# Two memsets moved, a third copy of the channel weights built by TensorE, and one weight load cut into seven

## The chip, the cores and the metric

The kernel runs on one core of a Trainium2 chip. The metric is the device time of one execution in microseconds; the figure given is the median of three runs. A profile of one further execution is used to say where the time goes; its times count from the start of its span.

## The reference

A causal convolution of seven taps, softmax-normalised and one set per head, is followed by a spectral mixing of the lowest 64 Fourier modes and a channel product with a ReLU:

```python
w = softmax(weight)                            # [8 heads, 7 taps]
x = causal_conv(x, w)                          # [8, 3264, 192], 24 channels a head
X = np.fft.rfft(x, axis=1)[:, :64]
Yr = Xr @ w_r - Xi @ w_i                       # per mode, 192x192
Yi = Xr @ w_i + Xi @ w_r
y = irfft(Yr + 1j*Yi, n=3264)                  # the other modes are zero
u = x + y
out = u + np.maximum(u @ w_ch, 0.0)            # w_ch is 192x192
```

All inputs and the output are float32; inside, the kernel works with bf16 operands and float32 accumulators.

## The kernel before

**Stages.** First, the taps are computed (VectorE and ScalarE, L231 to L241), TensorE spreads them into band matrices (L244), and copies put these into the tile `bandyet` (L249 to L253), which L187 has set to zero. Second, the convolution: the eight sequences are taken in four pairs, each in three units (`UNITS`), the last rows first. TensorE multiplies by the band matrices (L316 to L324), ScalarE and VectorE write the result back over `xall` (L331, L333), TensorE adds each finished unit to its Fourier transform with tables made on the fly (L341), and the result is transposed into `xt` (L355). The last 64 partitions of the last tile of every pair do not exist in the input; L188 sets them to zero. Third, the mixing: 16 groups of four modes. `mix(g)` (L463) multiplies `xt` by the weights of group g, 12 matmuls on L470. Between the groups, `some(3)` takes three bank jobs from a list, transposes by TensorE (L419, L429) with a copy each (L405, L407) that prepare tables `gt` and the transposed input `ct`; every second group ends in `mix_trans` (L485). Fourth, 52 output tiles: matmuls on L509, a ReLU (L539), an addition (L547) and a store by SP (L551).

**Channel weights.** `wm` holds rows 0 to 127 of `w_ch` and, in its columns 192 to 383, an identity; `w1` holds rows 128 to 191 and the remainder of that identity, on partitions 64 to 127. A third tile, `wch`, holds the same weights interleaved: partition p has rows 3p, 3p+1 and 3p+2, once on partitions 0 to 63 and once more on 64 to 127. The lower half is loaded (L284) and `spread_w` (L504, L505) copies it up by one VectorE copy of 64x576, called behind the mixing of groups 0 and 1. `wch` is first read by `z_c(0)`, ahead of the mixing of group 14.

**Order of the loads.** Every load of x and of weights is issued by POOL in the order of the program, since it turns float32 into bf16 on the way. The mixing weights of a group are two loads, real (w_r) into partitions 0 to 63 and imaginary (w_i) into 64 to 127 of a slot, of 288 KB each as written. Seven slots are used by 16 groups, so `load_free` issues the loads of a later group when the mixing that frees its slot has been written out: group 7's behind `mix(0)`, group 9's behind `mix(2)`, group 15's behind `mix(8)`. The program has 65 POOL loads: 30 of x, 3 of channel weights, 32 of mixing weights. Their completion is counted in eight semaphores, given out in turn (DMASW0 to DMASW7 in the built program), and each load waits, before it is issued, for the load that used its semaphore last, the eighth before it. Loads are called below by their part and group: r9 is w_r of group 9, i9 is w_i of group 9.

**Copies.** `copy` (L402) sends its second and fourth call of every five to ScalarE, the others to VectorE; `next_bank` (L409) turns through four PSUM banks.

Of the kernel before, what the change touches and what calls it, by code (L numbers as in the profile page):

```python
# [17 lines left out]
def kernel(  # L18
# [11 lines left out]
    nc = tc.nc  # L30
    B, S, D = x.shape
# [5 lines left out]
    P = 128  # L37
    NQ = B // 2
    NB = 13
# [25 lines left out]
    def sb(name, shape, dtype):  # L65
        return pool.tile([P] + shape, dtype, tag=name, name=name)
# [5 lines left out]
    xall = sb("xall", [NQ, NB, 2, 2, D], BF16)  # L72
# [5 lines left out]
    bandyet = sb("bandyet", [2 * H * P], BF16)  # L78
# [4 lines left out]
    wm = sb("wm", [2 * D], BF16)  # L83
    w1 = sb("w1", [2 * D], BF16)
    wch = sb("wch", [3, D], BF16)
# [7 lines left out]
    def wgroup(flat):  # L93
        return flat.rearrange("p (m j e) -> p m j e", m=4, j=3)

    slots = [wgroup(ct[:, 3, WGB * i:WGB * (i + 1)]) for i in range(4)]
    slots += [wgroup(arena[:, WGB * i:WGB * (i + 1)]) for i in range(NA)]
    NG = MODES // 4
    slot_of = [4, 5, 0, 1, 2, 3, 6, 4, 5, 0, 1, 2, 3, 6, 4, 5]
# [84 lines left out]

    blank = gt[:, :, :, :].rearrange("p h t s -> p (h t s)")[:, 0:512]
    nc.vector.memset(blank, 0.0)
    nc.vector.memset(bandyet[:], 0.0)  # L187
    nc.vector.memset(xall[64:P, :, NB - 1, 1, :, :], 0.0)  # L188
    nc.vector.memset(halfpi[:], math.pi / 2)
    nc.vector.memset(tiny, 0.0)  # L190
    nc.vector.memset(ascale[:], 2.0 / S)
# [2 lines left out]
    def active(n, bank, left, right):  # L194

        for _ in range(n):
            nc.tensor.matmul(bank[:, :], left, right, start=True, stop=True, skip_group_check=True)
# [41 lines left out]
    nc.vector.tensor_scalar(out=wsum[k7, :], in0=wsum[k7, :], scalar1=1e-9, scalar2=None, op0=ALU.add)  # L239
    nc.vector.reciprocal(out=wrec[k7, :], in_=wsum[k7, :])  # L240
    nc.vector.tensor_tensor(out=taps_t[k7, :], in0=wexp_t[k7, :], in1=wrec[k7, :], op=ALU.mult)  # L241

    for i in range(2 * PW):
        nc.tensor.matmul(xtrb[0:32, H * i:H * i + H], shift[k7, 2 * PW - 1 - i:2 * PW + 31 - i], taps_t[k7, :],  # L244
                         start=(i == 0), stop=True, tile_position=(0, 0), skip_group_check=True)
    for g in range(4):
        dst = band[32 * g:32 * g + 32, :, :, 16 * g:16 * g + PW]
        if g == 0:
            nc.vector.tensor_copy(out=dst, in_=xtrb[0:32, 0:2 * PW * H].rearrange("p (c e h) -> p e h c", e=2, h=H))  # L249
        elif g == 2:  # L250
            nc.scalar.copy(out=dst, in_=band[0:32, :, :, 0:PW])
        else:
            nc.vector.tensor_copy(out=dst, in_=band[0:32, :, :, 0:PW])  # L253
    active(6, dftb, blank[:, 0:P], blank)
    PIECES = ((18, 26), (10, 18), (0, 10))
    table_dve(*PIECES[0], (0, 1, 2))
# [24 lines left out]
        load_unit(*u)  # L281
    nc.gpsimd.dma_start(out=wm[:, 0:D], in_=moe_w_ch[0:P, :])
    nc.gpsimd.dma_start(out=w1[64:P, 0:D], in_=moe_w_ch[P:D, :])
    nc.gpsimd.dma_start(out=wch[0:64, :, :], in_=moe_w_ch.rearrange("(p j) e -> p j e", j=3))  # L284

    def load_w(g):
        for half, src in ((0, moe_w_r), (1, moe_w_i)):
            nc.gpsimd.dma_start(out=slots[slot_of[g]][64 * half:64 * half + 64, :, :, :],
                                in_=src[4 * g:4 * g + 4, :, :].rearrange("m (p j) e -> p m j e", j=3))

    loaded = [0]

    def load_free(mixed):
        while loaded[0] < NG:
            before = [g for g in range(loaded[0]) if slot_of[g] == slot_of[loaded[0]]]
            if before and before[-1] >= mixed:
                break
            load_w(loaded[0])
            loaded[0] += 1
# [102 lines left out]
    def copy(out, in_):  # L402
        ncopy[0] += 1
        if ncopy[0] % 5 in (2, 4):
            nc.scalar.copy(out=out, in_=in_)  # L405
        else:
            nc.vector.tensor_copy(out=out, in_=in_)  # L407

    def next_bank():  # L409
        k = tbank[0] % 4  # L410
        tbank[0] += 1
        return single[k][:, :]
# [44 lines left out]
    def some(n):  # L457
        for _ in range(n):
            if tjobs:
                f, *a = tjobs.pop(0)  # L460
                f(*a)

    def mix(g):  # L463
        last = g >= NG - 2
        yp = yps[g % 2][:, 0:D] if last else yps[(g // 2) % 2][:, D * (g % 2):D * (g % 2) + D]
        w = slots[slot_of[g]]
        for j in range(3):
            for p4 in range(4):
                m = 4 * g + p4
                nc.tensor.matmul(yp[32 * p4:32 * p4 + 2 * B, :], xt[:, j, :, m], w[:, p4, j, :],  # L470
                                 start=(j == 0 and (last or g % 2 == 0)), stop=(j == 2),
                                 tile_position=(0, 32 * p4), skip_group_check=True)
        mixed[0] = g
        load_free(g + 1)

    def mix_copy(d):
        nc.scalar.copy(out=ymix[d % 2][:], in_=yps[d % 2][:, 0:2 * D].rearrange("p (g d) -> p g d", g=2))
# [3 lines left out]
    def mix_trans(d):  # L481
        et = ets[d % 2][:, 0:256].rearrange("p (t g k) -> p t g k", t=2, g=2)
        for t in range(2):
            for g in range(2):
                nc.tensor.matmul(et[:, t, g, :], ymix[d % 2][:, g, 64 * t:64 * t + P], used, start=True,  # L485
                                 stop=True, skip_group_check=True)
        for t in range(2):
            yet_copy(d, t, et[:, t, :, :])
# [12 lines left out]
    def height(t):  # L501
        return P if t < NB - 1 else LASTM

    def spread_w():  # L504
        nc.vector.tensor_copy(out=wch[64:P, :, :], in_=wch[0:64, :, :])  # L505

    def z_mm(zt, e, i, l, r, begin, end):
        bank = zt[i] if isinstance(zt, list) else zt[:, i, :]
# [66 lines left out]
    for d in range(ND - 2):  # L575
        mix(2 * d)
        some(3)
        mix(2 * d + 1)
        mix_copy(d)
        some(3)  # L580
        mix_trans(d)
        if d == 0:
            spread_w()
        if d == 3:
            tjobs[5:5] = [(zw_job, q) for q in range(NQ)]
    d = ND - 2
# [80 lines left out]
    n = N - 1  # L667
# [6 lines left out]
    m = height(items[n][1])  # L674
# [38 lines left out]
```

## Time and profile before

| | |
|---|---|
| median of three runs | 175.78 us (175.54 to 175.99) |
| the profiled execution | 176.01 us |
| its span | 174.2 us, so 1.8 us lie outside it |
| granted TensorE clock | 0.993 |
| busy: PE, DVE, ACT, POOL | 157.3, 113.3, 98.4, 50.2 us |
| POOL's loads (q0, "software_dynamic") | 35600 packets, 19.62 MB |
| stores (q1, "hardware_dynamic") | 13934 packets, 20.06 MB |
| transfers of kind "instruction" on q8 | 24 packets of 16 KB |

The page cuts the span into 40 slices of 4.4 us; a digit is the busy share of a slice in tenths. POOL's loads run from 3 us to 105.7 us of the span, the stores from 111 us to the end. The groups, waits and timelines of the profile tell which instruction waited for what. Beside these the trace holds one row for each DMA packet (start, duration, size, queue, but not which of the 16 DMA engines moved it), and the time of each completion mark: each POOL load leaves sixteen, one by each DMA engine when its share has been written. A load has landed with its sixteenth mark.

### The profile page before, as it was taken

Reading aid. Unit: us, or ns where it says so; the run is one execution under the profiler, and the core shown is the slowest. Engines: PE = TensorE matmul, PEld = TensorE weight load, DVE = VectorE, ACT = ScalarE, POOL = GpSimd, SP = SyncE. Lnnn points to the kernel's source line nnn. Section 1 sums busy time; section 2 is a strip of 40 time slices with the busy share of each in tenths; the row PEclk is TensorE's granted clock in tenths of the full one; section 3 lists DMA queues with packets and bytes.
Section 4 is the critical chain, followed back from the end, with each engine's and each line's share of the span. In section 5 each row is a group of like instructions: output and inputs, shape, how many; then the busy total and the mean of one; then the engine's idle time right before and its main releaser. Section 6 shows DMA issues by size and latency. Waiting matters only on the chain.

```text
span 174.2 us, 7009 instructions
## 1 busy us (share of the span) xinstructions
PE 157.3 (90%) x3103; PEld 135.1 (78%) x3104; DVE 113.3 (65%) x158; ACT 98.4 (56%) x139; POOL 50.2 (29%) x82
## 2 busy tenths in 40 slices
PE   7669867999999999899999787999999999999970
PEld 2366746678888887688887774899999999999960
DVE  6697744254535435576775653887888888888880
ACT  3454737424444442658778572776667766676640
POOL 7985795444223642056444000000000000000000
PEclk9999999999999999999999999999999999999997
DMA  2999999999999999999999990299999999999985
GB/s 20 190 191 192 189 193 192 193 192 193 191 192 192 204 208 206 206 206 206 206 207 206 206 169 8 93 346 317 336 336 352 344 320 348 344 332 341 338 314 191
DMA packets 49627, 40.12 MB, mean 230 GB/s; under 512 B 28285, under 2 KB 49597, under 8 KB 49597
## 3 DMA queue, kind: packets, MB, share of 16 engines
q0 software_dynamic: 35600, 19.62, 81.1%
q1 hardware_dynamic: 13934, 20.06, 32.7%
q8 instruction: 24, 0.39, 0.8%
q14 instruction: 6, 0.05, 0.1%
q10 hardware_dynamic: 63, 0.00, 0.0%
HBM read 39.23 MB, written 20.05 MB: 340 GB/s over the span
## 4 chain that ended last, share of the span: by engine, by line
PE 71%; DMA 19%; POOL 4%; issue 2%; ACT 1%; DVE 1%; DVEq 0%; POOLq 0%
DMA xall<-in_x_dram 12%; PE x_right L341 9%; PE z_right L509 9%; PE zb_left L509 8%; PE zs L509 8%; PE zt L509 8%; PE w_left L429 7%; DMA arena<-in_moe_w_i_dram 6%; PE x_left L316 5%; PE x_left L321 3%; PE w_right L470 2%; PE x_right L316 2%; POOL xall L143 2%; PE w_left L419 2%; PE x_left L324 2%
## 5 line engine op out<-in xcount | busy, mean ns | idle before, releaser
L509 PEld LDWEIGHTS <-gt 64*128 64x128 bf16 (+1 forms) x832 | 35.5, 96 | 1.7 <-issue 1.5
L316 PEld LDWEIGHTS <-bandyet 128*64 128x64 bf16 x384 | 26.3, 110 | 11.2 <-issue 11.2
L316 PE MATMUL x_left<-xall,bandyet 128*64 128x192 bf16 (+1 forms) x256 | 25.6, 253 | 5.7 <-DMA xall<-in_x_dram 4.9
L333 DVE CAST xall<-x_left 128x768 bf16<-128x768 f32 (+1 forms) x16 | 16.1, 1007 | 18.6 <-PE x_left L324 13.3
L509 PEld LDWEIGHTS <-ct 64*128 64x128 bf16 (+1 forms) x624 | 26.5, 96 | 0.9 <-DVE ct L407 0.4
L143 POOL DMA_DIRECT2D xall<-in_x_dram x24 | 21.6, 909 | 13.2 <-DMA xall<-in_x_dram 12.5
L331 ACT CAST xall<-x_left 128x768 bf16<-128x768 f32 (+1 forms) x16 | 13.4, 838 | 20.2 <-PE x_left L324 20.2
L324 PE MATMUL x_left<-xall,bandyet 128*64 128x192 bf16 (+1 forms) x128 | 24.4, 251 | 0.0
L321 PE MATMUL x_left<-xall,bandyet 128*64 128x192 bf16 x128 | 23.7, 246 | 0.0
L321 PEld LDWEIGHTS <-bandyet 128*64 128x64 bf16 x192 | 21.1, 110 | 0.1
L324 PEld LDWEIGHTS <-bandyet 128*64 128x64 bf16 x192 | 21.1, 110 | 0.0
L407 DVE COPY ct<-w_left 128x1024 bf16<-128x1024 bf16 x24 | 15.9, 689 | 7.3 <-PE w_left L429 4.3
L429 PE MATMUL w_left<-ident,xall 128*128 128x128 bf16 x312 | 19.6, 220 | 0.0
L341 PE MATMUL x_right<-xall,fz 128*128 128x384 bf16 (+1 forms) x104 | 19.0, 327 | 0.0
L429 PEld LDWEIGHTS <-xall 128*128 128x128 bf16 x312 | 17.6, 103 | 1.7
L405 ACT COPY ct<-w_left 128x1024 bf16<-128x1024 bf16 (+1 forms) x16 | 15.2, 961 | 4.9 <-PE w_left L429 3.1
L333 DVE CAST xall<-x_right 128x768 bf16<-128x768 f32 (+1 forms) x8 | 8.5, 1057 | 9.9 <-PE x_right L324 7.7
L341 PEld LDWEIGHTS <-fz 128*128 128x128 bf16 (+1 forms) x104 | 9.4, 98 | 7.0 <-issue 0.7
L316 PE MATMUL x_right<-xall,bandyet 128*64 128x192 bf16 (+1 forms) x128 | 13.7, 257 | 0.8 <-DMA xall<-in_x_dram 0.8
L539 ACT ACTIVATE z_right<-z_right 128x768 f32<-128x768 f32 (+1 forms) x13 | 10.3, 794 | 4.8 <-PE z_right L509 4.3
L509 PE MATMUL zb_left<-fz,gt 64*128 64x192 bf16 (+1 forms) x208 | 13.0, 243 | 0.0
L324 PE MATMUL x_right<-xall,bandyet 128*64 128x192 bf16 (+1 forms) x64 | 13.0, 256 | 0.0
(130 smaller groups left out, 299.3 us busy)
## 6 DMA issues: line engine op xcount, KB each, us to landing
out_dram<-arena SPq DMA_DIRECT2D x25, 384.0 KB, 3.8
xall<-in_x_dram POOLq DMA_DIRECT2D x24, 384.0 KB, 12.4
out_dram<-xt SPq DMA_DIRECT2D x12, 384.0 KB, 3.7
out_dram<-ct SPq DMA_DIRECT2D x10, 384.0 KB, 3.5
arena<-in_moe_w_r_dram POOLq DMA_DIRECT2D x8, 288.0 KB, 10.4
arena<-in_moe_w_i_dram POOLq DMA_DIRECT2D x8, 288.0 KB, 10.3
ct<-in_moe_w_r_dram POOLq DMA_DIRECT2D x8, 288.0 KB, 9.9
ct<-in_moe_w_i_dram POOLq DMA_DIRECT2D x8, 288.0 KB, 10.7
```

What stands on the lines that cost most here:

```text
L143: nc.gpsimd.dma_start(out=dst, in_=src)
L316: nc.tensor.matmul(cols[r, :, e, :].rearrange("p t (i d) -> p t i d", i=2), band[:, e, h, 0:64], xall[:, q, t0:t0 + n, half, :, dsl], star ...
L321: nc.tensor.matmul(cols[0:64, b0:n, e, :].rearrange("p t (i d) -> p t i d", i=2), band[:, e, h, 64:P], xall[:, q, t0 + b0 - 1:t0 + n - 1, ...
L324: nc.tensor.matmul(cols[64:P, :, e, :].rearrange("p t (i d) -> p t i d", i=2), band[:, e, h, 64:P], xall[:, q, t0:t0 + n, 0, :, dsl], star ...
L331: nc.scalar.copy(out=dst, in_=srcv)
L333: nc.vector.tensor_copy(out=dst, in_=srcv)
L341: nc.tensor.matmul(xp, ftab[0:r, 2 * t + e, :], xall[0:r, q, t, e, :, :].rearrange("p i d -> p (i d)"), start=(t == UNITS[0][0] and e == 0 ...
L405: nc.scalar.copy(out=out, in_=in_)
L407: nc.vector.tensor_copy(out=out, in_=in_)
L429: nc.tensor.transpose(tp[:, P * k:P * k + P], src, ident[:])
L509: nc.tensor.matmul(bank[0:l.shape[-1], D * e:D * e + D], l, r, start=begin, stop=end, tile_position=(64 * i, 0), skip_group_check=True)
L539: nc.scalar.activation(out=zt[0:m, :, 0:2 * D], in_=zt[0:m, :, 0:2 * D], func=ACT.Relu)
```

## The change

Three edits:

1. The memset of `bandyet` moves from the head of VectorE's program to behind the last instruction of the taps (L241), and the memset of the missing rows of `xall` to behind the band copies (L253).
2. The load of `wch` and the copy in `spread_w` go. `channel_w`, called in the same place, makes `wch` from `wm` and `w1`: twelve matmuls whose stationary operand is every third column of the identity, over two PSUM banks, then two calls of `copy` (128x384 and 128x192).
3. r9 is issued as seven loads: its first three modes in one, and the rows of its fourth mode in six loads of 15, 14, 12, 10, 8 and 5 partitions.

```diff
     nc.vector.memset(blank, 0.0)
-    nc.vector.memset(bandyet[:], 0.0)
-    nc.vector.memset(xall[64:P, :, NB - 1, 1, :, :], 0.0)
...
     nc.vector.tensor_tensor(out=taps_t[k7, :], in0=wexp_t[k7, :], in1=wrec[k7, :], op=ALU.mult)
+    nc.vector.memset(bandyet[:], 0.0)
...
             nc.vector.tensor_copy(out=dst, in_=band[0:32, :, :, 0:PW])
+    nc.vector.memset(xall[64:P, :, NB - 1, 1, :, :], 0.0)
...
     nc.gpsimd.dma_start(out=w1[64:P, 0:D], in_=moe_w_ch[P:D, :])
-    nc.gpsimd.dma_start(out=wch[0:64, :, :], in_=moe_w_ch.rearrange("(p j) e -> p j e", j=3))
 
     def load_w(g):
         for half, src in ((0, moe_w_r), (1, moe_w_i)):
-            nc.gpsimd.dma_start(out=slots[slot_of[g]][64 * half:64 * half + 64, :, :, :],
-                                in_=src[4 * g:4 * g + 4, :, :].rearrange("m (p j) e -> p m j e", j=3))
+            n = 3 if g == 9 and half == 0 else 4
+            w = slots[slot_of[g]][64 * half:64 * half + 64, :, :, :]
+            nc.gpsimd.dma_start(out=w[:, 0:n], in_=src[4 * g:4 * g + n, :, :].rearrange("m (p j) e -> p m j e", j=3))
+            if n == 4:
+                continue
+
+            a = 0
+            for r in (15, 14, 12, 10, 8, 5):
+                nc.gpsimd.dma_start(out=w[a:a + r, 3, :, :],
+                                    in_=src[4 * g + 3, 3 * a:3 * (a + r), :].rearrange("(p j) e -> p j e", j=3))
+                a += r
...
-    def spread_w():
-        nc.vector.tensor_copy(out=wch[64:P, :, :], in_=wch[0:64, :, :])
+    def channel_w():
+
+        for js in ((0, 1), (2,)):
+            bank = next_bank()
+            for a, j in enumerate(js):
+                for i in range(2):
+                    for k, w in ((slice(0, P), wm), (slice(64, P), w1)):
+                        nc.tensor.matmul(bank[64 * i:64 * i + 64, D * a:D * a + D], w[k, D + j:2 * D:3], w[k, 0:D],
+                                         start=(a == 0 and w is wm), stop=(w is w1),
+                                         tile_position=(0 if w is wm else 64, 64 * i), skip_group_check=True)
+            copy(wch[:, js[0]:js[-1] + 1, :].rearrange("p j e -> p (j e)"), bank[:, 0:D * len(js)])
...
         if d == 0:
-            spread_w()
+            channel_w()
```

## The prediction

> **What bounds the kernel.** I read the page's slices first, then the chain of work that ended last, then the windows around the end of the loads, then POOL's timeline. In the page, DMA is at 9 from 4 us to 105 us, then nearly idle for two slices, then full again with the stores:
>
> ```profile
> DMA  2999999999999999999999990299999999999985
> ```
>
> The chain of work that ended last, cut to 88 to 112 us, ends its first part on a load:
>
> ```profile
> 93.35 0.61 POOL arena L288
> ...
> 94.53 11.20 DMA arena<-in_moe_w_i_dram
> 105.73 0.04 issue
> 105.77 0.47 PE w_right L470 x12
> ```
>
> i15 lands at 105.73 and the last mixing starts at once. From there to the end (174.2 - 105.73 = 68.47 us) the chain is TensorE's and the change touches none of it. So I forecast the landing of i15, and whether TensorE is ready for it. TensorE's timeline shows how far it is ahead:
>
> ```profile
> 97.17 0.45 PE L470 MATMUL w_right<-ct,xt 128*16 128x192 bf16 x12 [0.88 <-DMA ct<-in_moe_w_i_dram]
> 104.74 0.45 PE L470 MATMUL w_right<-arena,xt 128*16 128x192 bf16 x12
> 105.77 0.45 PE L470 MATMUL w_right<-arena,xt 128*16 128x192 bf16 x12 [0.58 <-DMA arena<-in_moe_w_i_dram]
> ```
>
> It waits 0.88 us for i12 and 0.58 us for i15; without waiting it needs 97.17 to 105.19 between them. The windows show that the sixteen DMA engines do not end together (next to last column DMA share, full at 1.21):
>
> ```profile
> 102.00:103.00 1.00, 0.50 (x16) 0.35 (x16) 0.64 (x2) 0.87 (x2) 0.00 (x0) 1.00 1.18 200
> 103.00:104.00 1.00, 1.00 (x22) 0.79 (x23) 0.00 (x0) 0.31 (x1) 0.00 (x0) 1.00 0.69 116
> 104.00:105.00 1.00, 1.00 (x30) 0.84 (x29) 0.29 (x1) 0.27 (x1) 0.00 (x0) 1.00 0.35 67
> 105.00:106.00 1.00, 0.42 (x24) 0.27 (x12) 0.00 (x0) 0.32 (x1) 0.00 (x0) 1.00 0.07 10
> ```
>
> The completion marks of i15 say the same: the first at 103.08, twelve by 104.36, four at 105.43 to 105.73. The first mark of r9 is at 84.47, so an engine does the 13 loads from i9 to i15 in 103.08 - 84.47 = 18.61 us, 1.43 a load. The late engines are those that a 16 KB transfer of kind "instruction" (q8; at 78.97, 85.25, 92.00, 98.45 us) went through: with each, one engine's marks move back by about 1.1 us and stay there.
>
> POOL's timeline shows what lets a load be issued:
>
> ```profile
> 78.48 0.61 POOL L288 DMA_DIRECT2D ct<-in_moe_w_r_dram  x1 [0.73 <-PE w_right L470]
> 79.08 0.62 POOL L288 DMA_DIRECT2D ct<-in_moe_w_i_dram  x1
> ...
> 88.80 0.61 POOL L288 DMA_DIRECT2D arena<-in_moe_w_i_dram  x1 [0.40 <-DMA ct<-in_moe_w_i_dram]
> ```
>
> 78.48 and 79.08 are r9 and i9, behind mix(2); 88.80 is i13, 0.28 after the last mark of i9, eight loads earlier, at 88.52. The same holds for i14 (91.68 after 91.40) and i15 (94.53 after 94.24). Eight loads in flight are 11.4 us of stock, so this never leaves an engine without work.
>
> **Edit 1, the zeros.** At the head VectorE has
>
> ```profile
> 1.30 0.91 DVE L187 MEMSET bandyet<- 128x1024 uint32 x1 [0.16 <-issue]
> 2.41 0.70 DVE L188 MEMSET xall<- 64x768 uint32 x1 [0.20 <-issue]
> 3.47 0.20 DVE L231 TENSOR_REDUCE ct<-ct 7x8 f32<-7x56 f32 x1
> ```
>
> Without them L231 can start when the weights land (marks to 2.61), so the taps come some 0.8 us sooner; TensorE takes them at 4.69, when its eight warm-up matmuls end, not at 5.16. The band copies end 0.47 sooner, at 6.93, the second memset brings the table work (L208, 7.43) to 7.67: 0.24 late. The first convolution waits for x until 9.28, and the chain still shows TensorE waiting for x at 29.26, so this is hidden. Value: nothing. Bounds: 0.24 worse, without that cover; 1.30 better, if the memsets now hold back the first descriptors (rival A).
>
> **Edit 2, the channel weights.** The load goes: the marks of its first engine are 56.96 for `w1` and 57.35 for `wch`, so every later load is 0.39 us earlier. TensorE gets twelve matmuls of 192 columns: 0.38 us at the rate of the mixing (12 in 0.38, L470 in the chain), 0.76 at that of the transposes (24 in 1.52, L429); I take 0.53 from the nearest shape, L437 at 192 columns (8 in 0.35, 107.27 to 107.62). The wait of 0.88 at i12 covers it. VectorE loses a 64x576 copy (0.42) and the two engines gain copies like L477 (0.48) and L618 (0.37); the shift in who copies what lies ahead of that wait too. Gain in the stream 0.39, cost nothing; if the wait were gone, 0.53 would go straight into TensorE's path.
>
> **Edit 3, the seven loads.** Six more issues at 0.53 (the `wch` row, L284) are 3.2 us of POOL. That is not the cost; the count is. r9 with its parts now takes seven of the eight semaphores, so i9 gets the one that i8 had, the load just before r9. The order of the built program confirms it: i8 and i9 both wait on DMASW1. i8's last mark was 85.68; less 0.39, 85.29; plus 0.28, POOL issues **i9 at 85.57, not 79.08**. In front of the engines lie then only r9 and its parts, one load, 1.43 us. The first engine ended i8 at 83.04 - 0.39 = 82.65 and is empty at 84.1; the last at 86.7.
>
> How long from an issue to its first packet, with an idle queue? Low end: SP's first store, issued 110.51, first packet 111.38: 0.87, without POOL's descriptor work. High end: the first load of x, issued 1.24, first packet 2.99, 1.75; the full packet rate came only at 4.15, 2.91. I take 1.33: the 0.61 of an L288 issue, and the 0.72 from the end of that first issue (2.27) to its first packet, since an L288 issue is shorter than an x one. [...]
>
> So i9 flows from 85.57 + 1.33 = 86.90 and all engines start it together: those that were 2.6 us ahead have lost their lead, and the slowest 0.2 us. Then 18.61 us for 13 loads: 105.51. The instruction transfers near 92.0 and 98.5 each fall on one engine and add 1.1: **106.61**. Before it was 105.73, so +0.88. What the six unequal parts do to the balance of the engines is lost in the restart.
>
> **Sum.** Span 174.2 + 0.88 = 175.08; with the 1.81 outside it, 176.89 against the profiled 176.01. That execution is 0.23 above the median shown, so the median forecast is 175.78 + 0.88 = 176.66, **176.7 us**. TensorE's path, with i12 landing at 86.90 + 7 x 1.43 + 1.1 = 98.0 and 8.02 behind it, is ready at 106.0 and does not bind. I call 0.3% (0.53 us) what a measurement can tell from no change.
>
> **Rivals.** *A, the stream starts sooner.* The first issue took 1.03 us against 0.89 for the others of its line, and the first packets trickle from 2.99 to 4.15, while the memsets end at 2.21 and 3.11. If they hold POOL's descriptors back, at most 0.14 + 1.16 = 1.30 us come back, everywhere: 176.66 - 1.30 = 175.36, not slower than before. It decides from 0.88 on. Against it: POOL's second issue ran beside the second memset in a usual 0.90, and the trickle outlasts both. [...]
>
> *B, no hole, and the parts balance the engines.* If i9's packets follow without a gap, the stream keeps the 0.39, and if part k falls on the first engines by number and the late ones are the last, the latest loses up to four rows of 89 ns, 0.36. That would land i15 at 104.98, so TensorE binds at about 105.21: 175.2. For it: the queue held five loads when r9 was issued. Against: i9's semaphore. [...] Which engine took what, this trace cannot show.
>
> *C, the hole is short.* With 0.87 from issue to packet the cost is 0.42: 176.2, within 0.3%; it decides below 0.98.
>
> **Chances.** Forecast 0.59 (slower). C 0.13 (within). A 0.14, of which 0.08 within and 0.06, together with a short hole, faster. B 0.14, half on either side of the 0.3% line. So faster 0.13, within 0.28, slower 0.59. The range takes in B at 175.2 and ends above at 177.3, past the price of 1.75 (177.1); only a start as slow as the first full rate (2.91 us, 178.2) lies beyond.
>
> **What would show it.** POOL issues i9 0.3 us after i8's last mark, near 85.6; the DMA share dips between 84 and 87 us, and after it the first marks of i9 lie together; i15 lands near 106.6; TensorE's wait there is 0.5 us or more. No dip, or a first packet well before 2.9 us, would make the forecast wrong.

## The result and the profile after

The changed kernel takes **178.32 us** (median of six runs, 178.10 to 178.49) against 175.68 for the kernel before in the same session (175.25 to 175.99): 2.64 us slower, ratio 1.0151, 95% interval 1.0136 to 1.0166. The forecast was 176.7 with a range to 177.3. The profiled execution took 178.39, its span 176.6, 2.4 longer than before.

The page's slices show where the time went before any other view:

```profile
DMA  2999999999999999999699992269999999999995
GB/s 22 190 191 192 189 193 192 192 193 192 191 193 195 203 209 206 206 207 204 87 166 207 206 206 48 68 233 348 338 335 345 342 343 359 344 341 327 346 327 195
```

In before the DMA row has 9 without a break up to the gap ahead of the stores. Now a 6 stands in the middle of it, and the rate falls there to 87 GB/s: a hole at 84 to 88 us. The windows over it (next to last column DMA share, 1.20 is full; last GB/s) show that it is two holes:

```profile
82.00:84.00 2.00, 2.00 (x50) 1.79 (x50) 1.38 (x3) 1.61 (x4) 2.00 (x5) 1.00 1.20 199
84.00:86.00 2.00, 2.00 (x49) 1.63 (x38) 1.56 (x4) 1.19 (x4) 1.11 (x2) 1.00 0.56 81
86.00:87.00 1.00, 1.00 (x23) 1.00 (x20) 0.39 (x2) 1.00 (x2) 0.29 (x2) 1.00 0.25 20
87.00:88.00 1.00, 1.00 (x26) 0.80 (x24) 0.87 (x2) 1.00 (x2) 1.00 (x3) 1.00 0.91 118
88.00:89.00 1.00, 1.00 (x19) 1.00 (x20) 0.76 (x3) 0.36 (x2) 1.00 (x2) 1.00 1.04 167
89.00:90.00 1.00, 1.00 (x25) 0.76 (x22) 0.80 (x2) 0.96 (x2) 0.72 (x2) 1.00 0.94 98
90.00:92.00 2.00, 2.00 (x44) 1.81 (x42) 1.48 (x4) 1.14 (x3) 1.93 (x4) 1.00 1.18 195
```

POOL's timeline has the issues around it:

```profile
80.83 0.62 POOL L289 DMA_DIRECT2D ct<-in_moe_w_r_dram  x1 [3.30 <-PE w_right L478]
81.44 3.04 POOL L295 DMA_DIRECT2D ct<-in_moe_w_r_dram  x6
85.38 0.64 POOL L289 DMA_DIRECT2D ct<-in_moe_w_i_dram  x1 [0.89 <-DMA arena<-in_moe_w_i_dram]
86.73 0.62 POOL L289 DMA_DIRECT2D ct<-in_moe_w_r_dram  x1 [0.71 <-PE w_left L437]
```

The six parts go out from 81.44; i9 follows at 85.38, 0.29 after the last mark of i8 (85.09), as forecast (85.57). r10, at 86.73, waited for the last mark of r9 (86.17), which had its semaphore before. Its row names a TensorE instruction as the releaser, but the issue comes 0.56 us behind that mark, and r13, r14 and r15 in before were each issued 0.53 us behind such a mark. The sixteen marks of i9, which in before were spread over 85.90 to 88.52, now lie between 89.02 and 89.26: the engines had run dry and started again together. i15 lands at 108.30 (before: 105.73).

TensorE's timeline shows the second thing that the forecast did not have:

```profile
77.50 0.29 PE L519 MATMUL w_left<-wm 128*64 128x192 bf16 x1
77.72 0.28 PE L519 MATMUL w_left<-w 64*64 64x192 bf16 x1
77.94 0.29 PE L519 MATMUL w_left<-wm 128*64 128x192 bf16 x1
...
80.07 0.45 PE L478 MATMUL w_right<-ct,xt 128*16 128x192 bf16 x12
...
99.76 0.45 PE L478 MATMUL w_right<-ct,xt 128*16 128x192 bf16 x12 [0.95 <-DMA ct<-in_moe_w_i_dram]
...
108.34 0.45 PE L478 MATMUL w_right<-arena,xt 128*16 128x192 bf16 x12 [0.44 <-DMA arena<-in_moe_w_i_dram]
```

The twelve channel matmuls start 0.215 us apart: 77.50 to 80.07, 2.57 us, not 0.53. TensorE still waits for i12 and for i15, so in this kernel the loads decide all the same.

The theory, **H**: r9 and its parts use up seven of the eight semaphores, i9 cannot be issued before i8 has landed, the loads stop and start again, and that is the loss. The rivals are: **T**, the slow matmuls; **P**, a cost of small loads by themselves; **U**, the unequal sizes; **V**, VectorE's copies that delay POOL's descriptors at the restart.

### The profile page after: what moved, and what is told of

It reads as the page before. It is cut to its first block, busy times and chain, and to the rows that moved or that the text cites. A ratio compares the mean times of both kernels' runs of the same rounds, so it can differ in the third digit from the quotient of the medians.

```text
span 176.6 us, 7048 instructions
## 1 busy us (share of the span) xinstructions
PE 159.9 (91%) x3115; PEld 136.4 (77%) x3116; DVE 112.7 (64%) x158; ACT 98.6 (56%) x140; POOL 52.9 (30%) x87
## 4 chain that ended last, share of the span: by engine, by line
PE 72%; DMA 18%; POOL 4%; issue 2%; ACT 1%; DVE 1%; DVEq 0%; POOLq 0%
DMA xall<-in_x_dram 12%; PE x_right L349 9%; PE z_right L526 9%; PE zb_left L526 8%; PE zs L526 8%; PE zt L526 8%; PE w_left L437 7%; DMA arena<-in_moe_w_i_dram 6%; PE x_left L324 5%; PE w_right L478 3%; PE x_left L329 3%; PE x_right L324 2%; POOL xall L143 2%; PE w_left L427 2%; PE x_left L332 2%
```

## The experiments

Median and ratio are against the kernel before on the same chip in the same session (175.43 to 175.55).

| run | what it is | us | ratio, 95% interval |
|---|---|---|---|
| zeros_only | edit 1 | 175.38 | 1.0001 (0.9991 to 1.0012) |
| chan_only | edit 2 | 176.24 | 1.0046 (1.0031 to 1.0062) |
| no_split | edits 1 and 2 | 176.38 | 1.0053 (1.0037 to 1.0068) |
| split_only | edit 3 | 179.09 | 1.0204 (1.0181 to 1.0227) |
| split_three | r9 in 1 + 3 loads | 175.49 | 1.0000 (0.9991 to 1.0009) |
| split_four | r9 in 1 + 4 loads | 176.74 | 1.0075 (1.0048 to 1.0102) |
| split_five | r9 in 1 + 5 loads | 177.60 | 1.0122 (1.0102 to 1.0143) |
| split_equal | r9 in 1 + 6 equal loads | 179.05 | 1.0214 (1.0177 to 1.0251) |
| quiet | split_only, no VectorE copy beside the restart | 179.81 | 1.0239 (1.0214 to 1.0263) |
| chan_full | edit 2, all matmuls over 128 rows | 175.09 | 0.9977 (0.9968 to 0.9987) |
| after_full | the change with chan_full's matmuls | 178.41 | 1.0186 (1.0144 to 1.0228) |
| best | edit 1 and chan_full | 175.15 | 0.9980 (0.9972 to 0.9989) |

**One edit at a time.** Each leaves the other edits of the diff above out.

zeros_only. 

> The kernel before with edit 1 alone. The first packet at 2.98 and the issue of the first load at 1.24 did not move in the changed kernel, so no gain from an earlier stream: within 0.3 us of before, 175.4 to 176.0. Rival A of the prediction (the memsets hold the first descriptors back): up to 1.3 us faster.

It is the same as before. The first packet of its loads comes at 2.99, as before. VectorE's timeline in the changed kernel has the taps ready at 4.1 instead of 5.1, but the table work behind the second memset starts at 8.09 instead of 7.43:

```profile
3.99 0.15 DVE L239 TENSOR_TENSOR ct<-ct 7x8 bf16<-7x8 f32 x1
4.31 0.91 DVE L240 MEMSET bandyet<- 128x1024 uint32 x1 [0.16 <-issue]
...
7.36 0.70 DVE L253 MEMSET xall<- 64x768 uint32 x1 [0.22 <-issue]
8.09 0.69 DVE L206 TENSOR_TENSOR ct<-ct 128x512 f32<-128x512 f32 x1
```

Neither shows further on: TensorE's first convolution starts at 9.27 there, against 9.31 before, and it still waits for x at 29.20. Rival A of the prediction is out: the loads gained nothing when the two memsets left their start.

chan_only. 

> The kernel before with edit 2 alone. As no_split if the zeros are worth nothing: the matmuls about 0.21 us apart, TensorE late by 2.3 us at mix(2), no wait left at i12 and i15, +0.9 us, 176.6. If the wait of 0.88 at i12 still covered them, as predicted: 175.3 to 175.7.

no_split. 

> Edits 1 and 2 without the cut of r9. Theory H (the hole in the loads, made by i9 waiting for i8's semaphore, is what costs): the DMA share shows no dip and i15 lands near 105.3. But the trace of the changed kernel also shows the twelve new matmuls 0.215 us apart, 2.57 us in all, so TensorE should be ready for the last mixing only near 106.7 (96.3 + 2.35 + 8.02) and decide: about +0.9 us on before, 176.6. Rival T (the matmuls alone cost the whole 2.6 us): +2.6, 178.3. Rival Z (nothing but the cut costs): 175.3 to 175.7.

Both are 0.8 to 0.95 slower, as H and the slow matmuls together had it. i15 lands early (105.13 in chan_only, 105.18 in no_split), and yet TensorE comes later still, without a wait; its line in no_split has the last two mixings in one piece:

```profile
96.67 0.45 PE L469 MATMUL w_right<-ct,xt 128*16 128x192 bf16 x12
98.51 0.45 PE L469 MATMUL w_right<-ct,xt 128*16 128x192 bf16 x12
103.36 0.45 PE L469 MATMUL w_right<-arena,xt 128*16 128x192 bf16 x12
106.20 0.70 PE L469 MATMUL w_right<-arena,xt 128*16 128x192 bf16 x24
```

So without the cut the bound changes hands: 2.57 us of matmuls eat the 0.88 of slack at i12 and come out behind the loads. T is real, but worth 0.8, not 2.6.

split_only. 

> The kernel before with edit 3 alone. Theory H: i9 issued near 85.9 (i8's last mark and 0.28), a gap in the stream to about 88, i15 landing near 108, +2.3 to +2.7 us, 178.0 to 178.4: the cut alone is enough for the whole loss. Rival T: no more than +0.5. A rival in which both add up: +1.7.

3.66 us slower in the median: the cut alone is enough for the whole loss. H is borne out, the size is above its range (the profiled execution, 178.56, was the quickest of the four; what the two longest have in common stands at the end of the next section). The same hole, at the same place:

```profile
84.00:86.00 2.00, 2.00 (x45) 1.81 (x43) 1.58 (x3) 1.13 (x3) 1.05 (x2) 1.00 0.72 114
86.00:88.00 2.00, 2.00 (x43) 1.76 (x41) 1.29 (x2) 1.76 (x4) 0.64 (x2) 1.00 0.58 61
88.00:90.00 2.00, 2.00 (x45) 1.81 (x43) 1.22 (x3) 1.70 (x3) 1.93 (x4) 1.00 0.96 135
```

**What in the cut costs.** The edit is the list of sizes alone, on the kernel before with edit 3:

```diff
-            for r in (15, 14, 12, 10, 8, 5):
+            for r in (24, 22, 18):                      # split_three
+            for r in (18, 16, 16, 14):                  # split_four
+            for r in (15, 14, 13, 12, 10):              # split_five
+            for r in (11, 11, 11, 11, 10, 10):          # split_equal
```

split_equal. 

> The kernel before with the fourth mode of r9 in six nearly equal loads (11, 11, 11, 11, 10 and 10 partitions). Theory H: the sizes do not matter, the restart puts all engines level, as split_only: 178.6 to 179.3. Rival U (the unequal sizes load the engines unevenly and cost or save something): another time by over 0.5 us.

The same as split_only: U is out, the unequal sizes neither help nor hurt here.

split_three. 

> The kernel before with r9 in four loads: three modes, then 24, 22 and 18 partitions of the fourth. i9 now shares a semaphore with r7, not i8. Theory H (the count of loads on eight semaphores makes the hole): i9 issued near 81.7, four loads of stock, no dip in the DMA share, all but a few tenths of the 3.7 us of split_only gone: 175.4 to 176.0. Rival P (small loads slow the stream by themselves, whatever waits): about half of the loss stays, 177.2.

Nothing is lost. i9 is issued at 81.43 and the windows of split_three show full DMA throughout:

```profile
82.00:84.00 2.00, 2.00 (x43) 1.76 (x41) 1.38 (x2) 1.35 (x3) 0.69 (x2) 1.00 1.21 206
84.00:86.00 2.00, 2.00 (x45) 1.81 (x43) 1.51 (x3) 1.23 (x2) 0.62 (x1) 1.00 1.21 203
86.00:88.00 2.00, 2.00 (x43) 1.76 (x41) 1.36 (x3) 1.67 (x4) 1.22 (x2) 1.00 1.22 206
```

Three small loads cost nothing that can be measured, so P is out as the cause.

split_four. 

> The kernel before with r9 in five loads (three modes, then 18, 16, 16 and 14 partitions). i9 waits for i7 and is issued near 83.1, running near 85.4, when every engine still has work. Theory H: as split_three, -0.2 to +0.4 us, 175.3 to 175.9. Rival P: +2.4, 178.0.

split_five. 

> The kernel before with r9 in six loads (three modes, then 15, 14, 13, 12 and 10 partitions). i9 then waits for r8, one load earlier than in split_only. Theory H, with 2.3 us from an issue to a stream at full rate as split_only and quiet showed: i9 issued near 84.5, running near 86.8; the engines that are ahead run dry for about a microsecond and lose their lead, the late ones do not; later instruction transfers then fall on engines without a lead: +0.5 to +1.3 us, 176.1 to 176.9. Rival P (a cost for each small load): five sixths of split_only's loss, +3.0, 178.5.

Both cost more than H had it, +1.2 and +2.1. The order is H's (0, 1.2, 2.1, 3.5 to 3.7 for three to six parts), the prices are not: I had counted one restart. In split_four i9 is issued at 82.94, when the first engines have 2 us of work left; they run dry for a few tenths, and then r10 (84.65), i10 (85.82) and r11 (87.47) each wait for the last mark of one of the three loads just ahead of the small ones (r8, i8 and r9). The first marks of i9, r10, i10, r11, i11, r12 and i12 are 86.67, 88.68, 90.15, 91.78, 93.35, 95.00 and 96.59: five of the six steps longer than the 1.43 of a load by 0.14 to 0.58. So the loss is spread over the loads from r10 to i12; it is not one gap. It is not only a lack of loads either: between 88 and 94 us the DMA share of split_four is 1.16 to 1.18, close to full, but the rate is 184 to 190 GB/s instead of 206, and a packet of 1152 bytes takes 112 to 117 ns on the mean of each of these microseconds, against 107 to 109 in split_three. Why the packets take longer is not shown.

**The way from an issue to a running stream.** quiet takes VectorE's wide copies away from the restart:

```diff
-        if ncopy[0] % 5 in (2, 4):
+        if ncopy[0] % 5 in (2, 4) or 5 <= mixed[0] <= 8:
             nc.scalar.copy(out=out, in_=in_)
```

> split_only, with all copies of the bank jobs behind the mixings of groups 5 to 8 on ScalarE, so that VectorE makes no wide copy while the loads start again. In split_only the first mark of i9 comes 3.72 us after its issue, 2.29 more than a load takes. Rival V (VectorE's copies hold back POOL's descriptors): it comes 0.6 to 1.0 us sooner and the second dip, ahead of r10, goes. Theory H0 (it is the way from an issue to a running stream, whatever VectorE does): 3.5 to 3.8 us as before. The total is not the point here, since ScalarE's copies are slower.

Its windows show VectorE at 0.00 and the hole still there:

```profile
86.00:88.00 2.00, 1.87 (x37) 1.51 (x35) 0.00 (x0) 2.00 (x4) 0.85 (x2) 1.00 0.38 36
88.00:90.00 2.00, 1.21 (x16) 0.93 (x15) 0.00 (x0) 2.00 (x4) 1.98 (x4) 1.00 1.06 130
```

From the issue of i9 to its first mark it is 3.64 us here, 3.65 in the changed kernel, 3.70 in after_full (below), 3.72 in split_only, 3.68 in split_equal, 3.69 in split_five, 3.73 in split_four. V is out. A load takes 1.43 of this, so 2.2 to 2.3 us pass from an issue to a stream at full rate. The packets of POOL's queue in steps of 0.2 us from the issue of i9, counted in the trace, show what these consist of (full is 35 to 37; packets of 4 bytes are left out; those ahead of 1.2 us are taken for the last of the small loads):

```
changed kernel   4  2  2  1  0  0  3 13 16 13  6 28 35 37 37
quiet            4  3  3  0  0  0  7 21  9  6 10 24 37 38 34
split_equal      5  3  4  4  1  1  6 13 10 11 11 28 38 35 35
```

The first packet of i9 comes after 1.2 us, some follow at a lower rate, then there is a lull, and only from 2.2 to 2.4 us on do they run at full rate.

**The matmuls.** chan_full makes both passes of a pair alike, over 128 rows; the rows of `w1` that come in hold zeros:

```diff
-                    for k, w in ((slice(0, P), wm), (slice(64, P), w1)):
+                    for k, w in ((slice(0, P), wm), (slice(0, P), w1)):
...
-                                         tile_position=(0 if w is wm else 64, 64 * i), skip_group_check=True)
+                                         tile_position=(0, 64 * i), skip_group_check=True)
```

> The kernel before with edit 2, but with both matmuls of each pair over all 128 partitions (those of w1 that hold zeros too) and at the same rows of the array. Rival R (the 0.215 us from matmul to matmul comes from changing between a pass over 128 rows and one over the upper 64): they come at 0.04 to 0.07 us, 0.5 to 0.8 us in all, the wait at i12 covers them and the 0.39 us of the load that went remains as gain: 175.0 to 175.3. Rival S (it comes from taking every third column as the stationary operand): as chan_only, 176.2.

0.46 us faster than before. TensorE's timeline:

```profile
77.67 0.29 PE L510 MATMUL w_left<-wm 128*64 128x192 bf16 x2
77.79 0.25 PE L510 MATMUL w_left<-w 128*64 128x192 bf16 x2
...
78.31 0.45 PE L469 MATMUL w_right<-ct,xt 128*16 128x192 bf16 x12
```

Twelve matmuls from 77.67 to 78.31, 0.64 us instead of 2.57, with the same stationary operand of every third column. S is out. That passes over 64 rows are not slow by themselves, at either half of the array, the kernel before shows: `z_c` alternates between the lower and the upper 64 rows, and twelve such passes of 192 columns start within 0.51 us (64*128 are the rows and columns of the array that a pass uses):

```profile
103.97 0.67 PE L509 MATMUL zb_left<-wch,ct 64*128 64x192 bf16 x12
104.48 0.33 PE L509 MATMUL zb_left<-fz,gt 64*128 64x192 bf16 x4
```

So R holds: where passes over 128 rows and over 64 alternate (chan_only), 0.215 us go by from start to start, against 0.05 with 128 rows throughout (chan_full) and 0.04 with 64 (before). What the array does in that time is not shown.

after_full. 

> The changed kernel with the twelve channel matmuls of chan_full (both of a pair over 128 partitions). If the hole in the loads covers what the slow matmuls cost, as the waits of TensorE at i12 and i15 in the changed kernel say (0.95 and 0.44 us): within 0.5 us of the changed kernel, 177.9 to 178.6. If both costs add up: 177.4 or less.

It takes as long as the changed kernel, 178.41: the costs of edits 2 and 3 do not add up. While the hole holds up the loads, TensorE has time for slow matmuls.

best. 

> Edit 1 and the channel weights as in chan_full, without the cut of r9: what is left of the change that is worth something. As chan_full, 0.3 to 0.5 us faster than before, 174.9 to 175.2, since the zeros are worth nothing. If moving the zeros costs or gains with them: outside of that.

175.15, 0.36 us faster than before, no better than chan_full: the load that went is the whole gain. In chan_full i15 lands 0.43 us earlier than in before, about what the kernel gains, and TensorE still waits 0.48 us for it.

## Why the prediction was wrong

**Edit 1, nothing:** right; zeros_only is the same within 0.12%. The table work came 0.66 us late instead of 0.24, under the same cover.

**Edit 2, gain 0.39, cost nothing:** the stream's gain is right (i15 lands 0.43 to 0.60 earlier in chan_full, chan_only and no_split). The cost of the matmuls was taken at 0.53 between 0.38 and 0.76; it is 2.57. The bounds came from rows in which all passes of a run have one shape, and this edit mixes two. Alone it turns the gain into a loss of 0.8 us (chan_only). In the full change it did not show, since the waits behind the hole cover it, so it is not what put the forecast out.

**Edit 3:** i9 waiting for i8, the restart of all engines together, the loss of their lead, and TensorE waiting at the end came as forecast. The step that failed is the term "I take 1.33" for the way from an issue to the stream. The first packet did come then (1.2 us), but 18.61 us of loads at full rate were counted from it, and full rate comes 1.0 us later. The prediction had that row in hand: the first load of x, first packet at 2.99, full rate at 4.15, put down as an upper end beyond the range. That this end, 178.2, lies close to the measured time is chance: with 2.21 for the term the prediction's sum gives 177.5, and most of the rest is a second hole, which it had put at nothing. The last mark of i15 by terms, forecast against trace:

| term | forecast | changed kernel | difference |
|---|---|---|---|
| issue of i9 | 85.57 | 85.38 | -0.19 |
| from there to the stream (first mark of i9, less 1.43) | 1.33 | 2.21 | +0.88 |
| i9 to i15 on an engine that met no instruction transfer | 18.61 | 19.37 | +0.76 |
| the engine that met one | 1.1 | 1.34 | +0.24 |
| last mark of i15 | 106.61 | 108.30 | +1.69 |

The 0.76 is the second hole: from the first mark of i9 to that of r10 it is 2.04 us, and 1.55 from there to that of i10, where a load takes 1.43. r10 waited for r9's last mark, 86.17, and its first mark came 4.33 us after its issue. The forecast had an answer for i9 alone; the loads behind it are bound by the semaphores too. The wait is not the whole of it: 2.21 us after its issue at 86.73, as i9 had it, r10 would have been there at 88.94, before the first engine was done with i9 (89.02). It took 2.90 (4.33 less 1.43), and why is not shown.

**Rivals.** A is out (zeros_only). B's condition never arose, since there was a hole; whether parts of just these sizes can balance the engines where no load waits for them was not tried (split_three, with 24, 22 and 18 partitions and no hole, is no faster than before). C, a short hole, is out: the way to the stream is 2.21 us, and the 0.87 that it rested on is a first packet too.

What stays open: why a few packets come first and then a lull follows. Only V was tried and excluded. That split_only is 0.8 us slower than the changed kernel in the median, of which the `wch` load that it still has could explain 0.39, is not settled either; in the two profiled executions i15 lands at 108.28 and 108.30. Two of the four executions of split_only had a granted TensorE clock of 0.973 and took 179.27 and 179.32; the other two, at 0.989 and 0.993, took 178.56 and 178.90, and the six of the changed kernel had 0.985 to 0.999. So the clock may be part of the difference; no run tests it.

## What to carry to other kernels

Count loads, not bytes, where completion semaphores go round: here one load cut into seven filled a window of eight, and the next load went out only 0.29 us behind the last mark of the load in front of the seven. Where a queue can run dry, price the restart to full rate (2.2 us here), not to the first packet (1.2 us), and follow the waits through the whole window. When a new matmul stands beside others, look for rows in which the same shapes alternate (0.215 us a matmul here); a run of equal shapes (0.05) says nothing of the change between two.

## What the runs showed of the hardware

- A POOL load into engines that run dry: 2.2 to 2.3 us from the start of its issue to a stream at full rate (first mark of i9 less 1.43, in seven runs), the first packet at 1.2 us in the three that are counted above; VectorE's copies make no difference to it (quiet).
- Alternating passes over 128 and over 64 rows: 0.215 us from matmul to matmul of 192 columns, against 0.05 with one shape (chan_only, chan_full), and 0.04 with 64 rows throughout (before).
- With a 16 KB transfer of kind "instruction" one of the sixteen marks of a load moves back by 1.1 us: in the kernel before, with the transfer at 78.97, the last mark of r7 is 81.36, where the last of i6, 78.82, and the 1.43 of a load give 80.25. Four marks that, by these steps, had moved back twice decided the landing of the last load (105.43 to 105.73; the twelve others were done by 104.36). That a mark stands for one DMA engine is my reading; the trace does not name the engine.
- A POOL load that waits for one semaphore is issued 0.28 to 0.29 us after the last mark (i13, i14 and i15 in before), one that has a slot to wait for too 0.53 to 0.56 us after it (r15 in before, r10 in the changed kernel).
